# The fourth second product of an MLP by pairs of token blocks, and the attention's division kept clear of the stage behind it

## The chip, the core and the metric

The kernel runs on one core of a Trainium2 chip. The metric is the device time of one execution in microseconds. TensorE (PE) does the matrix products, and its weight loads are shown apart as PEld. VectorE (DVE), ScalarE (ACT) and GpSimd (POOL) do the elementwise work, and SyncE (SP) issues every DMA of this kernel, one behind the other. Lines such as L646 are lines of the kernel before, unless the text says otherwise.

## The reference

The input x has 2048 tokens of 512 features. The output mixes an attention and an MLP of the same x with a gate:

```python
qkv = x @ wqkv                       # 32 heads of 16, scale 16**-0.5
mask = (i - j >= 0) & (i - j < 256)  # sliding window
a = softmax(where(mask, q @ k.T * scale, -1e9)) @ v     # per head
a = a @ wo
b = gelu_tanh(x @ w1 + b1) @ w2 + b2                    # 512 -> 1792 -> 512
g = sigmoid((x * gate_w).sum(-1))
out = g * a + (1 - g) * b
```

All of it is fp32.

## The kernel before, in words

**Dense products.** A dense product takes three matmuls, made by `mm3` (L108 to L110): each operand is split into a rounded part and the rest, and rounded by rounded, rounded by rest and rest by rounded are summed in PSUM. A weight tile therefore comes in as `raw_w` by DMA, ACT copies its rounded part into a `w` tile (L178) and DVE subtracts for the rest (L182). There are 14 `w` buffers and 2 `raw` buffers.

**The MLP in eight stages.** The tokens are cut into four tiles of 512, and the 1792 hidden features into two halves of seven blocks (`HF`). A stage n of the eight in `TURNS` takes one half for one tile: first the "u" part (seven blocks of x by w1, each followed by a chain for gelu on ACT and DVE, L719 to L737, that leaves a tile `h`), then the "y" part (four blocks b of 128 tokens, each the sum over seven i of h by w2). The fourth stage, n = 3, is the last that uses the first half of the weights. During its u part the loads of the second half of w1 are asked for, and in its y part one load of the second half of w2 is asked for behind each of the seven products of block b = 3 (L836). The fifth stage, n = 4, begins with the second half.

**The attention** goes by eight groups g of four heads and, within a group, by four chunks of 512 tokens. For each chunk PE makes row maxima's scores (`sm`, L519), which DVE reduces (`jm` and `M`, L524), then transposed scores (`st`, L564), on which ACT takes the exponential into `pt` (L586) and POOL clears what is outside the window (L580), and then the products with v (L608) into two PSUM tiles, `pv_st` and `pv_sm`. These two come from the same pools as `st` and `sm`, three buffers each. ACT copies the one into a tile `nd` (L629), DVE adds the other (L632), and SP stores the sum to DRAM as ND (L636). A name such as `nd4_1` is group 4, chunk 1.

**The division** (`att_norm`, L642) goes once per chunk and pair of groups, when the second group of the pair is stored: SP loads the denominators from ND (`den`, L646), DVE takes the reciprocal (L650), SP stores them (RD, L653), and later loads the numerators (`num`) and the reciprocals spread over the rows (`rb`, L658); DVE multiplies (L662), and SP stores the quotient (OT, L665), which only the last stage of the program reads. `den1_1`, `num1_1` and `rb1_1` belong to chunk 1 and the second pair of groups, which are groups 2 and 3. There is one `den` buffer, and `nd`, `num` and `rb` take turns in three buffers of one tag, `tmp`: whoever takes a buffer waits for the last reader of its former tile.

**What sets the order.** The order of instructions on each engine, SP among them, is the order in which the program records them; nothing reorders them later. The program keeps a clock of its own in planned nanoseconds. `after(ns, fn)` puts a piece of work on a list, and `tick` runs those whose time has come while PE's work is recorded (`fill` puts dense steps between the attention's). So the delays in the code are planned places in the order, and not waits on the chip. The division's steps are planned at 8, 10, 16, 23 and 25 us from its start (`DIVS`), and its start 6 us (`NORM`) after the store of ND. Weight loads are planned at least 4 us apart (`PACE`), with the split 7.5 us (`LAND`) after the load, and no more than two at a time, since there are two `raw` buffers (`load_now`).

**Semaphores of the DMAs.** SP's transfers use eight completion semaphores in turn, and the order's listing names the ones on which an instruction waits (DMAHW0 to DMAHW7).

## Time and profile before

| | us |
|---|---|
| time, median of 3 runs | 750.57 (749.57 to 752.2) |
| time of the profiled execution | 749.65 |
| span of the profiled execution | 747.9 |
| PE busy in it | 732.7 (98%) |
| DVE busy in it | 520.1 (70%) |
| ACT busy in it | 421.5 (56%) |
| POOL busy in it | 372.3 (50%) |
| share of the DMA queue that SP feeds | 81.4% of 16 engines |

A line of the profile gives a group of instructions or one instruction: its time, its engine, its source line, the tile written and the tiles read, and, in brackets or behind a bar, how long the engine stood idle ahead of it and who released it. Matmuls are pipelined, so a busy PE isn't PE at its peak. The places of this text are given in microseconds from the start of the span. The y part of the fourth stage begins at 391.9, the u part of the fifth at 427.6 and its y part at 463.7.

### The profile page before, as it was taken

How to read it: one execution, taken by the hardware profiler on the slowest of the kernel's cores; microseconds unless marked ns; L12 is line 12 of the kernel's file. 1: busy time of each engine (PE TensorE's matmuls, PEld its weight loads, DVE VectorE, ACT ScalarE, POOL GpSimd, SP SyncE). 2: the span in 40 equal slices, each digit the busy share in tenths (PEclk: the TensorE clock that was granted, in tenths of full speed). 3: DMA queues.
4: the chain of work that ended last, by engine and by line, in shares of the span. 5: the costliest groups of instructions: out<-in, count | busy, mean ns of one | idle time of the engine just before them, and what ended most of it. 6: DMA issues, size and time to landing. Idle time of an engine off the chain costs nothing.

```text
span 747.9 us, 17961 instructions
## 1 busy us (share of the span) xinstructions
PE 732.7 (98%) x6129; PEld 604.4 (81%) x6129; DVE 520.1 (70%) x1567; ACT 421.5 (56%) x972; POOL 372.3 (50%) x846
## 2 busy tenths in 40 slices
PE   8999999998999999999999999999999999999998
PEld 7888888876788888888887877888888888867786
DVE  4532325799768867986798689768867986784552
ACT  4434532358537845864695478438745863794550
POOL 4200000339756865876577568747765875630000
PEclk9999999999999999999999999999999999999999
DMA  9889798998895687899575979996799799468572
GB/s 326 319 272 404 261 391 273 291 293 182 270 259 134 162 243 205 175 222 271 146 179 149 242 211 234 249 237 152 178 256 235 194 224 270 136 181 226 191 252 111
DMA packets 179260, 172.12 MB, mean 230 GB/s; under 512 B 56673, under 2 KB 122977, under 8 KB 179169
## 3 DMA queue, kind: packets, MB, share of 16 engines
q1 hardware_dynamic: 179168, 170.97, 81.4%
q8 instruction: 49, 0.80, 0.5%
q14 instruction: 43, 0.34, 0.1%
HBM read 108.53 MB, written 62.39 MB: 229 GB/s over the span
## 4 chain that ended last, share of the span: by engine, by line
PE 85%; DVE 5%; ACT 3%; issue 3%; DMA 2%; SPq 1%; POOL 1%; DVEq 0%; ACTq 0%
PE sm L519 9%; PE st L564 8%; PE pv_sm L608 7%; PE y L108 7%; PE y L109 6%; PE y L110 6%; PE u L108 5%; PE u L109 5%; PE u L110 5%; PE qk L110 4%; PE qk L108 4%; PE qk L109 4%; PE a L108 2%; DVE jm L524 2%; PE v L108 2%
## 5 line engine op out<-in xcount | busy, mean ns | idle before, releaser
L524 DVE CUSTOM_DVE_ANT_0 jm<-sm,mask 128x320 bf16<-128x320 f32 (+4 forms) x512 | 238.1, 465 | 95.3 <-PE sm L519 61.1
L580 POOL TENSOR_SCALAR_AFFINE_SELECT pt<-pt 64x256 f32<-64x256 f32 (+1 forms) x538 | 227.7, 443 | 108.5 <-ACT pt L586 98.1
L586 ACT ACTIVATE pt<-st 128x320 f32<-128x320 f32 (+4 forms) x512 | 199.6, 424 | 139.1 <-PE st L564 136.0
L519 PE MATMUL sm<-kd,qd 96*128 96x320 f32 (+4 forms) x512 | 153.9, 312 | 6.3 <-DVE M L524 5.5
L564 PE MATMUL st<-qs,ks 128*128 128x320 f32 (+4 forms) x512 | 153.9, 309 | 1.9 <-ACT pt L586 1.9
L546 POOL CAST qs<-tt 4x256 fp32r<-4x256 f32 x256 | 124.6, 487 | 53.3 <-DVE tt L539 42.7
L519 PEld LDWEIGHTS sm<-kd,qd 96*128 96x128 f32 x512 | 96.3, 188 | 33.2 <-DVE M L524 13.7
L564 PEld LDWEIGHTS st<-qs,ks 128*128 128x128 f32 x512 | 97.1, 190 | 18.8 <-ACT pt L586 3.2
L108 PE MATMUL y<-w,h 128*128 128x512 f32 x224 | 88.5, 395 | 0.0
L109 PE MATMUL y<-w,h 128*128 128x512 f32 x224 | 87.9, 393 | 0.0
L110 PE MATMUL y<-w,h 128*128 128x512 f32 x224 | 87.9, 392 | 0.0
L108 PE MATMUL u<-mx,w 128*128 128x512 f32 x196 | 80.0, 408 | 0.0
L109 PE MATMUL u<-mx,w 128*128 128x512 f32 x196 | 77.4, 395 | 0.0
L110 PE MATMUL u<-mx,w 128*128 128x512 f32 x196 | 77.1, 393 | 0.0
L608 PE MATMUL pv_sm<-pt,vbuf 64*32 64x320 f32 (+4 forms) x1408 | 73.6, 346 | 0.2
L608 PE MATMUL pv_st<-pt,vbuf 64*32 64x320 f32 (+4 forms) x1408 | 73.3, 346 | 0.0
L608 PEld LDWEIGHTS pv_sm<-pt,vbuf 64*32 64x32 f32 x1408 | 50.2, 106 | 20.2 <-issue 2.4
L325 DVE TENSOR_TENSOR qke<-qk,qke 128x512 fp32r<-128x512 f32 x32 | 22.0, 688 | 46.9 <-ACT qke L322 33.2
L322 ACT ACTIVATE qke<-qk 128x512 fp32r<-128x512 f32 x32 | 19.1, 597 | 56.2 <-PE qk L110 32.5
L110 PEld LDWEIGHTS y<-w,h 128*128 128x128 f32 x224 | 42.0, 188 | 9.8
L338 POOL MEMSET vx<- 128x32 f32 x16 | 2.4, 156 | 89.0 <-DMA SQ<-qke 44.5
L608 PEld LDWEIGHTS pv_st<-pt,vbuf 64*32 64x32 f32 x1408 | 46.1, 106 | 0.0
(148 smaller groups left out, 1332.7 us busy)
## 6 DMA issues: line engine op xcount, KB each, us to landing
kd<-SK SPq DMA_DIRECT2D x32, 384.0 KB
qs<-SQ SPq DMA_DIRECT2D x64, 192.0 KB
mx<-XT SPq DMA_DIRECT2D x24, 512.0 KB
SQ<-qke SPq DMA_DIRECT2D x16, 512.0 KB
SK<-qke SPq DMA_DIRECT2D x16, 512.0 KB
ND<-nd SPq DMA_DIRECT2D x32, 256.0 KB
raw_w<-in_B_w_dram SPq DMA_DIRECT2D x28, 256.0 KB
ks<-SK SPq DMA_DIRECT2D x32, 192.0 KB
```

The lines of the kernel that those rows point to most:

```text
L108: nc.tensor.matmul(p, lh, rh, start=first, stop=False)
L109: nc.tensor.matmul(p, lh, rl, start=False, stop=False)
L110: nc.tensor.matmul(p, ll, rh, start=False, stop=last)
L322: nc.scalar.activation(e[:, h], p, AF.Copy)
L325: nc.vector.tensor_sub(e[:, 1 - h], p, f32(e[:, h]))
L519: nc.tensor.matmul(p[:, :w], qd[0:96, n, pr, 128 * j:128 * (j + 1)], kd[0:96, n, pr, k1 - w:k1], start=True, stop=True)
L524: nc.vector.tensor_tensor_reduce(junk[:, :w], p[:, :w], mask[:, 320 - w:320], 1.0, -3e38, ALU.add, ALU.max, M[:, 2 * (b % RB) + hb, pr:pr ...
L546: nc.gpsimd.tensor_copy(dst, src.unsqueeze(1).broadcast_to([4, 2, RB, 32]))
L564: nc.tensor.matmul(p[:, :w], ks[:, slot(g_, kb // NB), pr, at:at + 128], qs[:, pr, k0:k0 + w], start=True, stop=True)
L580: nc.gpsimd.affine_select(out=v, in_=v, pattern=[[0, v.shape[1]], [1 - 2 * e, 64]], compare_op=ALU.is_ge, fill=0.0, base=-e, channel_multi ...
L586: nc.scalar.activation(pt[:, hf, pr, :w], p[:, :w], AF.Exp, scale=SCALE)
L608: nc.tensor.matmul(pv[r // 64][32 * i:32 * i + 32, q - c * T:e - c * T], vts[g_, b // NB][r:r + 64, v:v + 32], rhs(r), start=start, stop=s ...
```

## The change

There are two edits. The y part of the fourth stage (n = 3) takes its 28 products in another order: block 0 and block 1 alternate from the fourth product on, then block 2 and block 3 likewise, where before only three products of block 1 stood ahead of block 0's last one, and blocks 2 and 3 came whole, one behind the other. Behind each product of block 3 a load of w2 is asked for, as before.

And the division is no longer started straight away 6 us after the store of ND. It goes through `norm`, which puts it off by 1 us again and again while `heavy` is set (from the beginning of that y part to the third block of the fifth stage's u part), and which starts two divisions at least 11 us of planned time apart (`APART`). `heavy` is never set elsewhere, and the last four divisions of the program don't go through `norm`.

```diff
--- before.py
+++ after.py
@@ -636,8 +636,21 @@
             nc.sync.dma_start(ND[c][g_ // 2][g_ % 2], nd)
             done.add(("nd", g_, c))
             if g_ % 2 == 1:
-                after(NORM if g_ * NT + c < NQ - 4 else 3500, att_norm, c, g_ // 2)
+                if g_ * NT + c < NQ - 4:
+                    after(NORM, norm, c, g_ // 2)
+                else:
+                    after(3500, att_norm, c, g_ // 2)
         after(100, half), after(700, ev)
+
+    norms = [0.0]
+
+    def norm(t, c):
+
+        at = max(now[0], norms[0])
+        if heavy[0]:
+            return after(1000, norm, t, c)
+        norms[0] = at + APART
+        after(at - now[0], att_norm, t, c)
 
     def att_norm(t, c):
 
@@ -739,6 +752,7 @@
         for ns, fn in zip(GELU, (f1, f2, f3, f4, f5, f6)):
             after(ns, fn)
 
+    heavy = [False]
     yas = {}
 
     def ya_load(k):
@@ -787,6 +801,8 @@
             hs.append(h)
             if last and later:
                 load(later.pop(0))
+            if n == NT:
+                heavy[0] = i < 2
         if n == 0:
             for c in range(NC):
                 nc.sync.dma_start(XT[t][c], f32(xt[:, c]))
@@ -823,8 +839,16 @@
 
 
         stage[0] = "y"
-        turns = [(0, i) for i in range(HF - 1)] + [(1, i) for i in range(YSWAP)] + [(0, HF - 1)]
-        turns += [(1, i) for i in range(YSWAP, HF)] + [(b, i) for b in range(2, NB) for i in range(HF)]
+        if n == NT - 1:
+            turns, heavy[0] = [], True
+            for b in range(0, NB, 2):
+                turns += [(b, i) for i in range(YSWAP)]
+                for i in range(YSWAP, HF):
+                    turns += [(b + 1, i - YSWAP), (b, i)]
+                turns += [(b + 1, i) for i in range(HF - YSWAP, HF)]
+        else:
+            turns = [(0, i) for i in range(HF - 1)] + [(1, i) for i in range(YSWAP)] + [(0, HF - 1)]
+            turns += [(1, i) for i in range(YSWAP, HF)] + [(b, i) for b in range(2, NB) for i in range(HF)]
         for b, i in turns:
             ts = slice(b * 128, (b + 1) * 128)
             if i == 0:
@@ -1002,6 +1026,7 @@
 GELU = (700, 1500, 3600, 4600, 6000, 7000)
 XAT = 3
 ORDER = 'mspf'
+APART = 11000.0
 XOR = 1
 PACE = 4000.0
 LAND = 7500.0
```

In the changed file the lines from `att_norm` to the end of `gelu` are higher by 13 (den L659, RD L666, num and rb L671, OT L678, mx L690, the gelu chain L732 to L750); those above are the same.

**DVE at the end of the fifth stage's u part.** Before, these rows follow one another; `jm` and `M` are one reduction of the score tile `sm`, and `w2_13` is the split of the last w2 tile:

```order
L524 ISA jm5_2_1_6706,M5_0_6520<-sm5_2_1_6704,mask_72 128x320
L524 ISA M5_0_6520 128x1
L524 ISA jm5_2_0_6722,M5_0_6520<-sm5_2_0_6720,mask_72 128x320
L524 ISA M5_0_6520 128x1
L182 TENSOR_TENSOR w2_13_6718<-raw_w213_6562,w2_13_6718 128x512
L524 ISA jm5_2_3_6734,M5_0_6520<-sm5_2_3_6732,mask_72 128x320
L524 ISA M5_0_6520 128x1
L731 SCALAR_TENSOR_TENSOR x1h2_12_6669_6675<-sqh2_12_6669_6676,x1h2_12_6669_6675 128x512
```

Now:

```order
L524 ISA jm5_2_1_6683,M5_0_6498<-sm5_2_1_6681,mask_72 128x320
L524 ISA M5_0_6498 128x1
L524 ISA jm5_2_0_6699,M5_0_6498<-sm5_2_0_6697,mask_72 128x320
L524 ISA M5_0_6498 128x1
L524 ISA jm5_2_3_6710,M5_0_6498<-sm5_2_3_6708,mask_72 128x320
L524 ISA M5_0_6498 128x1
L744 SCALAR_TENSOR_TENSOR x1h2_12_6647_6653<-sqh2_12_6647_6654,x1h2_12_6647_6653 128x512
L524 ISA jm5_2_2_6728,M5_0_6498<-sm5_2_2_6726,mask_72 128x320
```

The split of `w2_13` no longer stands among these reductions; it stands 16 rows ahead of the first row shown, and the splits of the other w2 tiles of this half have moved ahead likewise.

**SP from the y part of the fifth stage on.** Before, `RD3_1` is the store of the last of the four divisions, `mx40` parts of the next tile of x, `qs`, `kd` and `qd` loads of the attention:

```order
L653 DMA RD3_1_128<-den3_1_6494 128x32 [waits DMAHW1_49,DVE_49]
L677 DMA mx40_6739<-XT0_91 128x1024 [waits DMAHW2_49,PE_49]
L499 DMA qs_73<-SQ0_79 48x2x512 [waits DMAHW3_49]
L499 DMA qs_73<-SQ0_79 48x2x512 [waits DMAHW4_49]
L658 DMA num3_1_6814<-ND3_1_112 128x1x512 [waits DMAHW5_49]
L658 DMA rb3_1_6816<-RD3_1_128 128x1x512 [waits DMAHW7_49,DMAHW6_49,DMAHW1_49]
L677 DMA mx40_6739<-XT0_91 128x1024
L488 DMA kd_76<-SK1_84 96x2x256 [waits DMAHW0_49]
L488 DMA kd_76<-SK2_85 96x2x512 [waits PE_49]
L480 DMA qd_75<-SQ2_81 48x8x128 [waits DMAHW2_49]
L475 DMA qd_75<-SQ2_81 48x7x128 [waits DMAHW3_49]
L477 DMA qd_75<-SQ2_81 48x2x64 [waits DMAHW4_49]
```

Now the division of chunk 2 stands here, that of chunk 0 begins, and the store of chunk 1's quotient comes behind the loads:

```order
L690 DMA mx40_6715<-XT0_91 128x1024 [waits DMAHW6_49,PE_49]
L499 DMA qs_73<-SQ0_79 48x2x512 [waits DMAHW7_49]
L499 DMA qs_73<-SQ0_79 48x2x512 [waits DMAHW0_49]
L666 DMA RD2_1_124<-den2_1_6602 128x32 [waits DMAHW1_49,DVE_49]
L659 DMA den0_1_6795<-ND0_1_100 128x1x32 [waits DMAHW2_49,DMAHW1_49]
L690 DMA mx40_6715<-XT0_91 128x1024 [waits DMAHW3_49]
L488 DMA kd_76<-SK1_84 96x2x256 [waits DMAHW4_49]
L488 DMA kd_76<-SK2_85 96x2x512 [waits DMAHW5_49,PE_49]
L480 DMA qd_75<-SQ2_81 48x8x128 [waits DMAHW6_49]
L475 DMA qd_75<-SQ2_81 48x7x128 [waits DMAHW7_49]
L477 DMA qd_75<-SQ2_81 48x2x64 [waits DMAHW0_49]
L678 DMA OT1_96<-num1_1_6693 128x512 [waits DVE_49]
```

Of the divisions of these four chunks, which before started in the order 0, 1, 2, 3 during the fourth stage's y part and the fifth's u part, that of chunk 1 now starts first, behind the third block of the fifth stage's u part, and then those of chunks 2, 0 and 3. The load of `den0_1` waits for the store of RD that stands right ahead of it, since both use the one `den` buffer.

**ACT at the copy of `nd4_1`.** Before:

```order
L586 ACTIVATE pt4_8_6826<-st4_8_2_6858 128x320 [waits PE_49]
L629 ACTIVATE nd4_1_6918<-pv4_1_st_6863 128x512 [waits DMAHW0_49,PE_49]
L586 ACTIVATE pt4_8_6826<-st4_8_3_6923 128x320 [waits PE_49]
L586 ACTIVATE pt4_9_6950<-st4_9_0_6951 128x320 [waits PE_49,Pool_49]
L586 ACTIVATE pt4_9_6950<-st4_9_1_6958 128x320 [waits PE_49]
```

Now:

```order
L586 ACTIVATE pt4_8_6802<-st4_8_2_6835 128x320 [waits PE_49]
L629 ACTIVATE nd4_1_6900<-pv4_1_st_6840 128x512 [waits DMAHW1_49,DVE_49,PE_49]
L586 ACTIVATE pt4_8_6802<-st4_8_3_6905 128x320 [waits PE_49]
L586 ACTIVATE pt4_9_6931<-st4_9_0_6932 128x320 [waits PE_49,Pool_49]
L586 ACTIVATE pt4_9_6931<-st4_9_1_6939 128x320 [waits PE_49]
```

The copy takes a `tmp` buffer. Before, the last reader of that buffer was the store of an ND; now it is the store of `OT1_96` of the fence ahead, which uses DMAHW1, and which stands 8 rows of SP ahead of the store of `nd4_1` itself.

## The prediction, as it was put on record

> **What bounds the kernel now.** The page comes first.

> ```profile
> span 747.9 us, 17961 instructions
> PE 732.7 (98%) x6129; PEld 604.4 (81%) x6129; DVE 520.1 (70%) x1567; ACT 421.5 (56%) x972; POOL 372.3 (50%) x846
> ```

> PE is the bound; only what makes PE wait counts. [...] What PE waited for over the span, from the view of waits:

> ```profile
> PE sm L519 <- DVE M L524: 5.5, 11, 1.0
> PE st L564 <- ACT pt L586: 1.9, 3, 1.2
> ...
> PE a L108 <- DVE ao L879: 0.2, 1, 0.2
> ```

> The columns are total us, count and longest; these are the first two and the last of eight rows. The largest is the wait for the row maxima, 5.5 of 747.9 us, and none of the eight is a y or u matmul that waits for a weight tile. The places of the change were then read by stretches: an untouched y stage, the y part of the fourth stage, and the u and y parts of the fifth.

> ```profile
> core 0: us, PE busy (x) PEld busy (x) DVE busy (x) ACT busy (x) POOL busy (x), PEclk, DMA share, GB/s
> 288.90:323.60 34.70, 34.70 (x324) 28.82 (x323) 29.63 (x95) 26.93 (x61) 24.74 (x52) 1.00 0.75 167
> 391.90:427.80 35.90, 34.69 (x343) 28.61 (x342) 27.36 (x91) 18.27 (x44) 25.31 (x61) 1.00 0.74 184
> 427.80:463.50 35.70, 34.64 (x317) 27.59 (x317) 32.03 (x97) 28.27 (x64) 24.52 (x48) 1.00 0.85 223
> 463.50:498.00 34.50, 33.77 (x339) 27.58 (x338) 25.35 (x86) 16.47 (x40) 23.78 (x59) 1.00 1.00 255
> ```

> The granted clock is full. DVE is fullest in 427.8 to 463.5 (32.03 of 35.70). The DMA engines are fullest in the stretch behind it (1.00, 255 GB/s): that is where the divisions go. PE's waits in the three last stretches, the first row from 391.9 to 427.8, the next two from 427.8 to 463.5, the last from 463.5 to 498:

> ```profile
> PE sm L519 <- DVE M L524: 1.2, 2, 0.9
> ...
> PE sm L519 <- DVE M L524: 0.4, 2, 0.3
> PE sm L519 <- DVE nd L632: 0.4, 1, 0.4
> ...
> PE sm L519 <- DVE M L524: 0.6, 1, 0.6
> ```

> All six end on DVE, 2.6 us. That is all that this change can win here.

> **The change part by part. Turns by pairs.** The 28 products and their matmuls are the same, so PE work changes by 0. Block 3's products come four products earlier, and so each of the seven w2 loads and splits. As PE waits for no weight, the earlier buffers alone bring 0; the cover is that no such wait is there. What they do is take DVE work out of the end of the fifth stage's u part:

> ```profile
> 440.75 0.75 DVE L662 TENSOR_TENSOR num<-num,rb 128x512 f32<-128x512 f32 x1 [0.48 <-DMA rb<-RD]
> 443.58 0.42 PE L519 MATMUL sm<-kd,qd 96*128 96x320 f32 x1 [0.26 <-DVE M L524]
> 458.69 0.36 PE L519 MATMUL sm<-kd,qd 96*128 96x192 f32 x1 [0.43 <-DVE nd L632]
> 460.10 0.89 DVE L662 TENSOR_TENSOR num<-num,rb 128x512 f32<-128x512 f32 x1
> 461.32 0.41 PE L519 MATMUL sm<-kd,qd 96*128 96x320 f32 x1 [0.17 <-DVE M L524]
> 464.85 0.69 DVE L182 TENSOR_TENSOR w<-raw_w,w 128x512 fp32r<-128x512 f32 x1
> 465.86 0.69 DVE L731 SCALAR_TENSOR_TENSOR x1h<-sqh,x1h 128x512 f32<-128x512 f32 x1
> 466.88 0.85 DVE L725 SCALAR_TENSOR_TENSOR sqh<-sqh,x1h 128x512 f32<-128x512 f32 x1
> 467.11 0.32 PE L519 MATMUL sm<-kd,qd 96*128 96x320 f32 x1
> 467.26 0.31 PE L564 MATMUL st<-qs,ks 128*128 128x320 f32 x1
> 468.19 0.41 PE L519 MATMUL sm<-kd,qd 96*128 96x320 f32 x1 [0.62 <-DVE M L524]
> ```

> Three of these waits have a cause that moves. At 468.19 PE waits behind the split of w2_13 at 464.85 (0.69 us) and two gelu steps; without the split, the 0.62 goes. At 443.58 and 461.32 it waits 0.26 and 0.17 behind a division's multiply (440.75, 460.10), which moves. The wait at 458.69 stays: the order puts w2_13 where w2_12 stood, beside that `nd`. A wait is longer than its bracket, since a matmul of 0.31 us follows its forerunner after 0.15 (467.11, 467.26): 0.16 is hidden each time. Gain: 0.26 + 0.17 + 0.62 + 3 x 0.16 = **1.5 us**. Its bounds: 0, if other DVE work falls on the same places, and 2.6 + 6 x 0.16 = 3.6, if all six waits go.

> **The division moved.** Its instructions are the same and each issue costs SP the same; it leaves DVE idle earlier and busy later, and the multiplies come where DVE has 9 us free (25.35 of 34.50). Its transfers move into the stretch where the DMA share is 1.00. Two waits are new there. The load of `den0_1` has to wait for RD2's landing (one buffer), and so holds all of SP; and the copy of `nd4_1` on ACT has to wait for OT1's landing, since the `tmp` buffer that it takes is now num1's. Behind that copy stand the exponentials on ACT, and PE's fourth `st` behind it needs the PSUM tile that the copy frees. Rows of before for this place:

> ```profile
> 433.07 7.66 DMA rb<-RD
> 447.88 3.07 DMA raw_w<-in_B_w_dram
> ...
> 474.83 0.60 ACT L629 ACTIVATE nd<-pv_st 128x512 f32<-128x512 f32 x1 [1.94 <-PE pv_sm L608]
> 475.54 0.68 DVE L632 TENSOR_TENSOR nd<-nd,pv_sm 128x512 f32<-128x512 f32 x1
> ...
> 476.91 0.31 PE L564 MATMUL st<-qs,ks 128*128 128x320 f32 x1
> ...
> 462.64 0.40 SPq L653 DMA_DIRECT2D RD<-den  x1
> 463.61 0.32 SPq L677 DMA_DIRECT2D mx<-XT  x1
> ...
> 466.29 0.45 SPq L677 DMA_DIRECT2D mx<-XT  x1
> 466.79 2.16 SPq L488 DMA_DIRECT2D kd<-SK  x2
> 468.99 0.45 SPq L480 DMA_DIRECT2D qd<-SQ  x1
> ...
> 470.51 0.43 SPq L677 DMA_DIRECT2D mx<-XT  x1
> ```

> The first two are transfers of 0.26 MB in the chain that ended last, with issue to landing: 3.07 us in a calm queue, 7.66 in a loaded one. SP's rows give about 0.5 us for an issue.

> *Landing of RD2.* It is issued behind `num1`, `rb1`, a part of mx (463.61, 0.8 us earlier by the gain up to there: 462.8) and two loads of qs, so at 464.3. By the calm row it lands at 467.4; by the loaded one, counted from `rb1` at 462.1, rb1 lands at 469.8, and behind it come mx and qs, 0.92 MB at 255 GB/s = 3.6 us, 473.4. I take 471, since rb1, the slow one, stands ahead of it.

> *Landing of OT1.* Then come den0, mx, kd, kd, three qd and OT1. The seven issues after den0 take 3.5 us. Their bytes are 0.52 + 0.20 + 0.39 + 0.20 + 0.17 + 0.03 + 0.26 = 1.77 MB, at 255 GB/s 6.9 us, and the calm row leaves 3.07 - 0.26/0.255 = 2.0 us beside the bytes. From the issue of mx at 471.6: 471.6 + 6.9 + 2.0 = 480.5. The bounds from RD2's go from 476.9 to 482.9. SP also waits for the transfer eight issues before its own; before, that cost 2.1 us in this place, and it can only make OT1 later:

> ```profile
> SPq L480 <- DMA rb<-RD: 2.1, 1, 2.1
> ```

> *The stall A.* The copy ends 0.6 us later, at 481.1. The `st` that needs it would come at 476.91 - 1.5 = 475.4. **A = 5.7 us**, between 2.1 and 8.1. [...]

> *Behind it, B and C.* The same happens to `nd4_2`, one chunk later: nd4_0's add ended near 458.69, nd4_1's at 476.22, so the pitch is 17.5 and nd4_2's copy is due at 474.83 + 17.5 + 4.2 = 496.5. It waits for OT2. SP stores nd4_1 at about 481.8, then RD0, and is held at den3 until that lands (3.07 to 7.66 later: 485 to 489.5); six more issues, 3 us, then OT2 lands 3.07 to 7.66 later: 491 to 500. B is 0 to 3.5. C is the fuller queue: 1.5 divisions more in the last stretch, each 3 x 0.26 MB at 255 GB/s = 3.1 us, so 0 to 4.7, for the loads are asked for a chunk (17.5 us) ahead. I take 2.0 for both, nearer to the low ends, with 0 and 5 as bounds.

> The wait of den2 for RD1 near 455 costs SP up to 7.66 us too, and holds the loads of ks behind it; the cover is again that chunk ahead, and I put it at 0, and at what exceeds 17.5 us if it is gone.

> Sum against the profiled execution, 749.65: - 1.5 + 5.7 + 2.0 = 755.85. The median of the runs shown is 0.92 above that execution, so **756.8 us**.

> **The rivals.** *Clean gain.* OT1 lands ahead of the copy, as its like did before. For it: the copy then waited only for PE (1.94, 474.83). Against it: OT1 would have to land by 474.8, and even the low bound is 476.9. The time is 749.65 - 1.5 + 0.92 = 749.1, and with all six waits gone 747.0. It decides if SP isn't held at den0 for more than 2 us. What counts as faster, below, needs a gain over 2.25.

> *A small stall.* RD2 lands early and the queue is emptier than its share says: A is 2.1 to 3, B and C 0, so the time is 751.2 to 752.1, no change. For it: the calm row. Against it: 1.00 and 7.66.

> *A second stall of the same size.* `nd4_2` waits as long as `nd4_1`: with B at 3.5 and C at 4.7 instead of 2.0 it is 763.0. For it: two more divisions cross the same full stretch. Against it: after the first stall everything has 4.2 us more.

> *The change doesn't do what it says.* The splits move but others take their place, no wait goes: the gain is 0 and the time 1.5 higher with A, 758.3. It lies in the likeliest case's range.

> **How the numbers follow.** A measurement of this kernel can't tell less than about 0.3%, 2.25 us, from no change: 748.3 to 752.8. The likeliest case (stall A, 753 to 761) has 0.64; the small stall 0.12 and the clean gain at 749.1 0.04, both no change; the clean gain with more waits gone 0.10, faster; the second stall 0.10. So faster 0.10, no change 0.16, slower 0.74. The range of 8 in 10 reaches from 750.0, where the small stall begins, to 763.5 behind the second.

> **What would show it.** In the changed kernel's profile: PE waits of several us at `st` L564 between 475 and 482, put down to ACT; ACT's `nd` L629 there with idle time ended by the DMA of OT; SP waiting at `den` for the DMA of RD; the stretch from 463.5 longer by 6 or more us, the one from 427.8 shorter by about 1; no wait at 468.19. The prediction is wrong if `nd4_1`'s copy waits for PE alone, or if the time comes from a load of `ks`, `kd` or `mx` that is late.

## The result, and the profile after

The changed kernel takes 760.61 us in the median of 6 runs (757.08 to 761.95), the kernel before 750.74 us beside it (749.57 to 752.2). The ratio is 1.013, with a 95% interval of 1.0106 to 1.0155: it is slower, as forecast, by 9.9 us where 6.2 were forecast, and inside the range of 750.0 to 763.5. Its profiled execution is the fastest of the six, 757.08 us; the five others lie between 760.3 and 762.0, and that spread has a cause of its own, below.

The page after: the span, the busy times, and the two groups that changed.

```profile
span 755.4 us, 17970 instructions
PE 734.3 (97%) x6129; PEld 606.1 (80%) x6129; DVE 520.6 (69%) x1567; ACT 421.8 (56%) x972; POOL 370.7 (49%) x846
...
L564 PE MATMUL st<-qs,ks 128*128 128x320 f32 (+4 forms) x512 | 154.6, 310 | 8.3 <-ACT nd L629 6.1
...
L629 ACT ACTIVATE nd<-pv_st 128x512 f32<-128x512 f32 x32 | 19.1, 597 | 50.9 <-PE pv_sm L608 35.9
```

No engine is busier than before. The idle time ahead of `st` has grown from 1.9 to 8.3 us, and 6.1 of it is put down to ACT's `nd`. The waits of PE over the span (total us, count, longest) say that it is one wait:

```profile
PE st L564 <- ACT nd L629: 6.1, 1, 6.1
PE sm L519 <- DVE M L524: 5.5, 10, 1.0
```

The stretches, with the granted clock (the share of its full clock that TensorE was granted) in the third column from the end. The last is taken longer, since the stage ends later:

```profile
427.80:463.50 35.70, 35.39 (x326) 29.20 (x325) 32.70 (x101) 29.13 (x66) 24.61 (x50) 1.00 0.80 186
463.50:505.00 41.50, 34.84 (x334) 28.67 (x333) 25.42 (x87) 15.37 (x39) 21.97 (x56) 0.92 0.80 213
```

The first of the two is better filled than before (PE busy 35.39 instead of 34.64, and 9 matmuls more done in it): the gain is there. In the other the clock is no longer 1.00. The place itself, first in the timeline (start, us, engine, instruction, in brackets the idle time ahead of it and who ended it), with the rows of SP, ACT and PE one behind the other:

```profile
469.99 0.59 SPq L659 DMA_DIRECT2D den<-ND  x1
...
474.18 0.43 SPq L678 DMA_DIRECT2D OT<-num  x1
...
480.39 0.60 ACT L629 ACTIVATE nd<-pv_st 128x512 f32<-128x512 f32 x1 [9.62 <-DMA OT<-num]
...
466.06 0.41 PE L519 MATMUL sm<-kd,qd 96*128 96x320 f32 x1 [0.56 <-DVE M L524]
...
481.04 0.64 PE L564 MATMUL st<-qs,ks 128*128 128x320 f32 x1 [6.10 <-ACT nd L629]
```

And in the waits of SP between 450 and 500:

```profile
SPq L659 <- DMA RD<-den: 9.4, 3, 4.7
```

This is the forecast chain: SP is held 4.7 us at the load of `den0_1`, which goes at 469.99; OT1 goes at 474.18; the copy of `nd4_1` has waited 9.62 us for its landing and starts at 480.39; PE's `st` comes at 481.04 after 6.10 us of idle time. The matmul at 466.06 is the one that stood at 468.19 before, so the kernel was 2.1 us ahead there.

Behind the stall PE runs at half its clock (columns: PE busy, weight loads, DVE, ACT, POOL, then clock, DMA share, GB/s):

```profile
478.00:479.00 1.00, 0.00 (x0) 0.00 (x0) 0.00 (x0) 0.00 (x0) 0.00 (x0) 0.86 1.13 335
479.00:480.00 1.00, 0.00 (x0) 0.00 (x0) 0.00 (x0) 0.00 (x0) 0.00 (x0) 0.50 1.11 373
...
485.00:486.00 1.00, 1.00 (x4) 0.73 (x4) 0.01 (x1) 0.00 (x0) 0.95 (x3) 0.72 1.00 275
486.00:487.00 1.00, 1.00 (x7) 0.94 (x6) 0.50 (x3) 0.49 (x2) 0.18 (x1) 1.00 0.48 114
```

To book the time, I compare the starts of the same `st` matmul in both traces. Up to 468 the changed kernel is 2.1 us ahead. Behind the stall it is 6.3 us late, so the stall costs 8.4: 6.1 of idle time, and 2.3 for the 4.5 us in which PE works at 0.50. Near 510 comes 1.3 more. The sum, -2.1 + 8.4 + 1.3 = 7.6, is but for 0.2 the difference of the profiled executions, 757.08 - 749.65 = 7.4.

### The profile page after: what moved, and what is told of

Same layout as the page of the kernel before. It is cut to its first block, busy times and chain, and to the rows that moved or that the text cites. A ratio compares the mean times of both kernels' runs of the same rounds, so it can differ in the third digit from the quotient of the medians.

```text
span 755.4 us, 17970 instructions
## 1 busy us (share of the span) xinstructions
PE 734.3 (97%) x6129; PEld 606.1 (80%) x6129; DVE 520.6 (69%) x1567; ACT 421.8 (56%) x972; POOL 370.7 (49%) x846
## 4 chain that ended last, share of the span: by engine, by line
PE 85%; DVE 4%; ACT 3%; DMA 3%; issue 3%; SPq 1%; POOL 1%; DVEq 0%; ACTq 0%; POOLq 0%
PE sm L519 9%; PE st L564 8%; PE pv_sm L608 7%; PE y L108 6%; PE y L109 6%; PE y L110 6%; PE u L108 6%; PE u L109 5%; PE u L110 5%; PE qk L110 4%; PE qk L108 4%; PE qk L109 4%; PE a L108 2%; PE v L108 2%; PE v L110 2%
## 5 line engine op out<-in xcount | busy, mean ns | idle before, releaser
L524 DVE CUSTOM_DVE_ANT_0 jm<-sm,mask 128x320 bf16<-128x320 f32 (+4 forms) x512 | 238.1, 465 | 94.3 <-PE sm L519 59.8
L586 ACT ACTIVATE pt<-st 128x320 f32<-128x320 f32 (+4 forms) x512 | 199.6, 425 | 138.8 <-PE st L564 135.3
L564 PE MATMUL st<-qs,ks 128*128 128x320 f32 (+4 forms) x512 | 154.6, 310 | 8.3 <-ACT nd L629 6.1
L519 PE MATMUL sm<-kd,qd 96*128 96x320 f32 (+4 forms) x512 | 153.8, 312 | 6.0 <-DVE M L524 5.5
L519 PEld LDWEIGHTS sm<-kd,qd 96*128 96x128 f32 x512 | 96.6, 189 | 31.8 <-DVE M L524 11.9
L564 PEld LDWEIGHTS st<-qs,ks 128*128 128x128 f32 x512 | 97.5, 191 | 25.7 <-ACT nd L629 6.4
L108 PE MATMUL y<-w,h 128*128 128x512 f32 x224 | 89.2, 398 | 0.0
L108 PE MATMUL u<-mx,w 128*128 128x512 f32 x196 | 80.0, 408 | 0.0
L608 PE MATMUL pv_sm<-pt,vbuf 64*32 64x320 f32 (+4 forms) x1408 | 73.6, 346 | 0.1
L608 PE MATMUL pv_st<-pt,vbuf 64*32 64x320 f32 (+4 forms) x1408 | 73.3, 346 | 0.0
L608 PEld LDWEIGHTS pv_sm<-pt,vbuf 64*32 64x32 f32 x1408 | 50.2, 106 | 20.2 <-issue 2.2
L629 ACT ACTIVATE nd<-pv_st 128x512 f32<-128x512 f32 x32 | 19.1, 597 | 50.9 <-PE pv_sm L608 35.9
```

The lines of the kernel that those rows point to most:

```text
L108: nc.tensor.matmul(p, lh, rh, start=first, stop=False)
L519: nc.tensor.matmul(p[:, :w], qd[0:96, n, pr, 128 * j:128 * (j + 1)], kd[0:96, n, pr, k1 - w:k1], start=True, stop=True)
L524: nc.vector.tensor_tensor_reduce(junk[:, :w], p[:, :w], mask[:, 320 - w:320], 1.0, -3e38, ALU.add, ALU.max, M[:, 2 * (b % RB) + hb, pr:pr ...
L564: nc.tensor.matmul(p[:, :w], ks[:, slot(g_, kb // NB), pr, at:at + 128], qs[:, pr, k0:k0 + w], start=True, stop=True)
L586: nc.scalar.activation(pt[:, hf, pr, :w], p[:, :w], AF.Exp, scale=SCALE)
L608: nc.tensor.matmul(pv[r // 64][32 * i:32 * i + 32, q - c * T:e - c * T], vts[g_, b // NB][r:r + 64, v:v + 32], rhs(r), start=start, stop=s ...
```

## The experiments

Each run was taken beside runs of the kernel before on the same chip; the ratios are to those, with their 95% intervals in brackets. Runs on different chips are compared by their ratios. The diffs show the lines that matter; "..." stands for lines left out.

**The turns alone.** The division starts as before:

```diff
-                if g_ * NT + c < NQ - 4:
-                    after(NORM, norm, c, g_ // 2)
-                else:
-                    after(3500, att_norm, c, g_ // 2)
+                after(NORM if g_ * NT + c < NQ - 4 else 3500, att_norm, c, g_ // 2)
```

> The pair turns alone, the divisions started as before. Theory (all of the loss is one stall of PE: ACT's copy of nd4_1 waits for the landing of OT1, and the granted clock is low for some 5 us behind it): the copy waits for PE alone, the wait of 0.62 us at 468.19 behind the split of w2_13 goes, so 0 to 1 us faster than before: 749.5 to 751. Rival (the turns themselves cost, by crowding weight loads): about 757 to 760.

Measured: 750.27 us in the median against 750.12, ratio 1.0004 (0.9988 to 1.0021). The turns cost nothing and bring nothing that can be measured. By the starts in the trace this kernel is 0.5 us ahead at 468. It was 0.4 us behind already from 160 on, where both kernels are the same, so from 391.9 on the turns win 0.9 us, but not where I expected it. PE's instruction there, in this run's timeline:

```profile
467.71 0.41 PE L519 MATMUL sm<-kd,qd 96*128 96x320 f32 x1 [0.61 <-DVE M L524]
```

The matmul of 468.19 still waits 0.61 us, although the split of w2_13 is no longer among DVE's work ahead of it. The two gelu steps there (0.69 and 0.85 us, with the reductions behind them) are enough.

**The division alone.** The fourth stage has its old turns:

```diff
-            turns, heavy[0] = [], True
+            heavy[0] = True
+            turns = [(0, i) for i in range(HF - 1)] + [(1, i) for i in range(YSWAP)] + [(0, HF - 1)]
+            turns += [(1, i) for i in range(YSWAP, HF)] + [(b, i) for b in range(2, NB) for i in range(HF)]
```

> The division put off as in the changed kernel, the fourth stage's turns as before. Theory: the same stall of about 6 us at the copy of nd4_1 with a low clock behind it, plus the 0.6 to 0.8 us at w2_13's split that the turns would have taken away: 758 to 762. Rival (the turns cost): near 750.

Measured: 759.21 us, ratio 1.0118 (1.0085 to 1.0151). Its trace has the same stall, by the waits of PE from 463.5 to 520:

```profile
PE st L564 <- ACT nd L629: 6.1, 1, 6.1
```

So the whole loss belongs to the division that was put off, and the turns have no part in it. At 468 this kernel is 1.6 us ahead; counted from 391.9, where it was 0.5 us behind, it wins 2.1. The changed kernel wins 2.2 from there (2.2 to 2.6 in the seven traces with the same work up to 468), so the shares of the division and of the turns don't simply add.

**A buffer of its own for `nd`.** One of the three `tmp` buffers goes to `nd`, two stay for `num` and `rb` (the loads of x for the last stage, which use these buffers too, are shared out likewise):

```diff
-        nd = sb.tile([128, T], F32, tag="tmp", bufs=3, name=f"nd{g_}_{c}")
+        nd = sb.tile([128, T], F32, tag="nd", bufs=1, name=f"nd{g_}_{c}")
...
-                tiles.append(sb.tile([128, T], F32, tag="tmp", bufs=3, name=f"{name}{t}_{c}"))
+                tiles.append(sb.tile([128, T], F32, tag="tmp", bufs=2, name=f"{name}{t}_{c}"))
```

> The changed kernel, with one of the three buffers of tmp given to nd alone, and the other two to num and rb; SP is still held at den0 for RD2, and rb2 now has to wait for OT1. Theory: the copy of nd4_1 waits for PE alone, the stall and the low clock behind it go, and what is left is the gain: 748.5 to 751. Rival (SP's being held at the den loads, and with it late loads, costs the time): still 756 to 761.

Measured: 760.24 us, ratio 1.0117 (1.0093 to 1.0141). My expectation missed, and the rival, a late load behind SP's being held, comes nearer. The copy of `nd4_1` waits for PE alone now, but the wait for OT1 has only moved to the load of `rb2`. The waits of SP between 455 and 510 in this run:

```profile
SPq L671 <- DMA OT<-num: 9.5, 2, 5.2
```

And one instruction each of DVE and PE in its timeline:

```profile
484.16 0.69 DVE L675 TENSOR_TENSOR num<-num,rb 128x512 f32<-128x512 f32 x1 [5.25 <-DMA rb<-RD]
...
485.32 0.63 PE L519 MATMUL sm<-kd,qd 96*128 96x320 f32 x1 [4.16 <-DVE M L524]
```

SP is held 5.2 us at the load of `rb2`, DVE stands at the multiply for it, the reductions stand behind the multiply, and PE waits 4.16 us for a reduction, with the half clock behind it. In both arrangements of the buffers someone waits for OT1.

**Two `den` buffers.** This takes away SP's wait for RD2; the space for it comes from the table `cut`, which is bf16 now:

```diff
-        den = sb.tile([128, 32], F32, tag="den", bufs=1, name=f"den{t}_{c}")
+        den = sb.tile([128, 32], F32, tag="den", bufs=2, name=f"den{t}_{c}")
...
-    cut = cs.tile([128, 2, 64], F32, name="cut")
+    cut = cs.tile([128, 2, 64], BF16, name="cut")
```

> The changed kernel with two den buffers (96 bytes for it come from the table cut, now bf16), so that den0 no longer waits for RD2 and SP isn't held 4.7 us there; the copy of nd4_1 still waits for OT1. Theory (OT1 is late since its issue is late): OT1 is issued some 4 to 5 us earlier and lands at 475 to 477, the stall is 0.5 to 2 us: 750.5 to 753.5. Rival (the queue is full, and OT1 lands at 479 to 480 whenever it is issued): the stall stays 5 to 6 us, 757 to 761.

Measured: 751.38 us, ratio 1.0019 (0.9992 to 1.0046); nine of ten executions lie between 749.4 and 754.9, one at 759.61 (its mean clock is 0.993, as in the stalled executions of the changed kernel). The waits of PE from 463.5 to 520 show that the stall has shrunk:

```profile
PE st L564 <- ACT nd L629: 1.5, 1, 1.5
```

The mean clock of the execution is 1.0. OT1's issue and the copy in this run:

```profile
470.65 0.34 SPq L678 DMA_DIRECT2D OT<-num  x1
...
476.49 0.60 ACT L629 ACTIVATE nd<-pv_st 128x512 f32<-128x512 f32 x1 [5.02 <-DMA OT<-num]
```

OT1 goes 3.5 us earlier than in the changed kernel, and the copy starts 3.9 us earlier. (The rest of the 4.6 us by which the stall is shorter is that PE was 0.7 us later in this execution.) So OT1 was late because SP was held, and not because the queue was full whenever it was issued; from its issue to the copy it takes 5.8 us here and 6.2 there. This is the change's first cause: the 11 us between two divisions' starts leave 1 us between the store of RD (10 us after the start) and the load of the next `den` into the same buffer.

**PE kept busy over the wait, and the changed kernel again.** The score matmul ahead of the waiting `st` is issued 40 times, with the same result; the wait for OT1 stays.

```diff
+        for _ in range(40 if (g_, b, i) == (5, 5, 0) else 1):
-        nc.tensor.matmul(p[:, :w], qd[0:96, n, pr, 128 * j:128 * (j + 1)], kd[0:96, n, pr, k1 - w:k1],
+            nc.tensor.matmul(p[:, :w], qd[0:96, n, pr, 128 * j:128 * (j + 1)], kd[0:96, n, pr, k1 - w:k1],
...
```

> The changed kernel, where the score matmul that stands ahead of the waiting st (0.15 us each) is issued 40 times over into the same tile, so that PE is busy during the some 6 us in which it waits for the copy of nd4_1. The wait for OT1 stays as it is. Theory (of the 8.4 us lost there, 6.1 are the wait and 2.3 the granted clock of 0.5 behind it): the clock stays at 1.0, and the time is 2 to 3 us below the changed kernel's, 754.5 to 758. Rival (the low clock belongs to the work behind the wait, not to the idle time): no gain, 757 to 762.

> The changed kernel once more, as a base for the run ahead, and for a second trace: its six executions lay at 757.1 once and at 760.3 to 762.0 five times. If the place where the low clock begins makes that difference, the stall is the same 6 us and the clock of 0.5 lies wholly on busy time, up to 3.4 us instead of 2.3. If a second wait makes it, the trace shows another idle time of PE of 2 to 4 us.

Measured: 761.93 us (ratio 1.0148, 1.0126 to 1.017) with PE kept busy; 760.51 us (1.012, 1.0093 to 1.0148) for the changed kernel. In the first the clock holds at the stall, as two stretches over the stall and behind it show (the clock is the third column from the end):

```profile
478.00:480.00 2.00, 2.00 (x16) 2.00 (x15) 0.00 (x0) 0.00 (x0) 0.00 (x0) 1.00 1.00 330
...
482.00:484.00 2.00, 2.00 (x11) 1.76 (x12) 1.86 (x7) 1.49 (x5) 1.56 (x4) 1.00 1.01 196
```

The stall costs 6.1 us by the `st` starts there, instead of 8.4: the 2.3 is the clock's. But the gain is given back in the next 30 us (2.0 near 497 and 1.5 near 510, where the changed kernel's profile has 0 and 1.3): near 497 DVE stands 1.84 us at a multiply for `rb`, and PE behind it. Nor is the clock full everywhere in this kernel: the mean of the traced execution is 0.998, although the stretches read from 470 to 496 and from 512 to 528 all have 1.00, and the mean clocks of the four executions are 0.995 to 0.998.

The second trace of the changed kernel is an execution of 760.57 us, and shows what makes the spread. Its stall at `nd4_1` is 6.6 us long. Near 516, DVE stands at the last division's multiply, and PE behind it. The timeline of the first trace:

```profile
514.66 0.69 DVE L675 TENSOR_TENSOR num<-num,rb 128x512 f32<-128x512 f32 x1 [2.86 <-DMA rb<-RD]
...
516.42 0.41 PE L519 MATMUL sm<-kd,qd 96*128 96x320 f32 x1 [0.45 <-DVE M L524]
```

That of the second:

```profile
516.52 0.69 DVE L675 TENSOR_TENSOR num<-num,rb 128x512 f32<-128x512 f32 x1 [4.10 <-DMA rb<-RD]
...
518.28 0.42 PE L519 MATMUL sm<-kd,qd 96*128 96x320 f32 x1 [1.69 <-DVE M L524]
```

And the second trace's stretches there:

```profile
518.00:520.00 2.00, 1.41 (x6) 0.93 (x6) 1.71 (x5) 2.00 (x5) 0.58 (x2) 0.95 1.14 251
520.00:522.00 2.00, 2.00 (x6) 1.71 (x7) 1.86 (x8) 1.67 (x4) 1.71 (x4) 0.50 1.14 324
522.00:524.00 2.00, 2.00 (x10) 1.86 (x9) 1.49 (x5) 0.87 (x2) 0.35 (x1) 0.69 1.05 216
```

When DVE's wait for `rb` is 1.2 us longer, PE waits 1.69 us instead of 0.45, the clock falls a second time, and the place costs 4.0 us instead of 1.3. The mean clocks of the ten executions of the changed kernel fit this: 0.995 in the two at 757, and 0.992 or 0.993 in seven of the eight at 760 and more (the eighth has 0.996).

**The last multiply later.** Two runs test that: the changed kernel with one multiply recorded behind 7 more reductions, and, as the price of the low clock was still mixed with the second stall, the same with PE kept busy as above.

```diff
+        late = 4000 if (t, c) == (3, 1) else 0
         for ns, fn in zip(DIVS[c == NC - 1], (rcp, keep, back, mul, store)):
-            after(ns, fn)
+            after(ns + late * (fn in (mul, store)), fn)
```

> The changed kernel with the multiply and the store of the last of the four divisions (chunk 3) recorded 4 us of planned time later, behind 7 more reductions of DVE. Theory (the executions at 760 us and more are those in which rb of that division lands later, DVE stands at the multiply, PE waits 1.7 us for the row maxima and the clock falls once more): the wait near 516 is gone and with it the spread, and all executions lie at 755.5 to 757.5. Rival (the spread comes from the first stall): the median stays at 760 to 761.

> Both edits on the changed kernel: the score matmul issued 40 times ahead of the waiting st, and the last multiply 4 us later. With PE kept busy alone the median was no lower than the changed kernel's, since the second stall was still in it; without that stall the price of the low clock stands alone. Theory (2 to 3 us of the first stall are the clock of 0.5 behind it): 2 to 3 us below the run with the late multiply alone (756.46), 753.5 to 755. Rival (the low clock costs nothing, as what it delays had slack): 756 to 757.

Measured: 756.46 us (756.1 to 759.05; ratio 1.0083, 1.006 to 1.0107) for the first. PE has no wait between 505 and 520, and three of four executions lie within 0.7 us. All four have a mean clock of 0.995. So the second stall makes most of the difference between 757 and 761: 2.8 of 3.5 us between the two traces of the changed kernel (0.8 is there already from 160 on).

With PE kept busy as well: 757.67 us (754.96 to 761.55; 1.0071, 1.0049 to 1.0093). The intervals overlap, so no gain is shown. The three fastest of its seven executions (754.96 to 755.46) lie 0.6 to 1.1 us below the fastest without it, the others above. Its trace, an execution at 761.55, has 3.7 us from an undisturbed part of the kernel near 205, no loss to the clock at the stall, and 3.9 us behind it, at what is 497 in the kernel before. Only part of that is a new wait; the half clock comes back behind it, as one row of the timeline and one stretch show (the kernel's lines are higher by one in this run):

```profile
505.91 0.41 PE L520 MATMUL sm<-kd,qd 96*128 96x320 f32 x1 [1.72 <-DVE M L525]
...
507.45:510.86 3.41, 3.41 (x12) 2.83 (x11) 2.46 (x9) 0.72 (x3) 0.82 (x2) 0.50 0.92 182
```

DVE had stood 2.58 us at the multiply for `rb` ahead of it. The six other executions have a mean clock of 0.999 or 1.000, and still lie between 754.96 and 757.89. That the low clock costs 2.3 us where it stands is shown; that its removal would shorten the kernel is not. In the two traces with PE kept busy, waits for `rb`, and in the second the half clock behind one, took the gain back.

**More room between the divisions.** APART is 16000 instead of 11000, with the pair turns and with the old ones:

```diff
-APART = 11000.0
+APART = 16000.0
```

> The changed kernel with APART = 16000 instead of 11000: each division's transfers fall between two copies of nd, so that nd4_1 takes the buffer of nd4_0, and den0 is loaded 4 us or more behind the store of RD2. Theory: no wait of ACT for an OT, no stall, the gain of 2.1 us up to 468.19 stays, and some of the 1.1 us near 510: 748.5 to 750.5. Rival (the divisions' transfers in the full stretch cost by themselves): 752 or more.

> As the run before, with the old turns in the fourth stage's y part. Theory: the shares of the gain add up, 1.6 us of the moved divisions and 0.5 of the turns, so this is 0.5 us slower than with the pair turns: 749 to 751. Rival (the turns are worth nothing, or the gain is theirs): the same as with the pair turns, or as the kernel before.

Measured: 750.14 us against 750.68 (0.9992, 0.9975 to 1.0009) with the pair turns, and 748.98 us (0.9978, 0.9968 to 0.9988) with the old ones. Neither has a wait of ACT for an OT, nor a low clock at this place: with one number of the change its loss is gone. That the old turns do no worse here went against my expectation; that they do better is not shown, since the intervals overlap. In the traces the pair turns lose it near 508, where PE waits 1.45 us for a reduction, behind a multiply that waits 3.90 for `rb`; with the old turns the multiply waits 2.83. Why `rb` is later with the pair turns was not tried. Some 0.5 us of the gain lies elsewhere, in all three traces with 16000: near 324, ahead of the fourth stage's y part, since APART spaces the earlier divisions too.

**And later multiplies.** The same, with the old turns:

```diff
+        late = {mul: 2500, store: 1500} if c == 1 else {}
         for ns, fn in zip(DIVS[c == NC - 1], (rcp, keep, back, mul, store)):
-            after(ns, fn)
+            after(ns + late.get(fn, 0), fn)
```

> APART = 16000, the old turns, and the four divisions' multiplies recorded 2.5 us and their stores 1.5 us of planned time later. Theory (what is left in that kernel is DVE standing 2.8 us at a multiply for rb near 504, which takes back about 1 us of its gain): 747 to 748.5, 0.3 to 0.4% faster than the kernel before. Rival (the multiplies then stand at places where DVE is full): 749 to 751.

Measured: 748.25 us against 751.02, ratio 0.997 (0.9955 to 0.9985), with a span of 746.5 in the profiled execution. This is the lowest median of the study, and faster than before; that it is faster than the run without the later multiplies is not shown, since the intervals overlap. One division's multiply still waits 2.47 us for `rb`.

## Why the prediction was right, and where it was not

The direction and the cause were right: the copy of `nd4_1` waits for OT1, since SP is held at `den0` and a buffer has another last reader. The steps:

- *RD2's landing, 471, and OT1's, 480.5.* The load behind RD2 went at 469.99, and the copy started at 480.39. That the second is right to 0.1 us is partly luck: RD2 was 1.0 us earlier than taken, and the way from there to OT1's landing took 10.4 us instead of 9.5.
- *The stall A, 5.7.* The wait is 6.1. The term was too small nevertheless, and this is the step of the sum that failed, since a whole price was missing: the granted clock falls during the wait, and PE works at 0.50 for 4.5 us behind it, 2.3 us. The stall costs 8.4. I wrote that the clock is full, and did not ask what a wait would do to it. In this trace the clock falls 3.8 us into the idle time, at 478.72.
- *B and C, 2.0 with bounds 0 and 5.* The size holds: 1.3 in the one trace, 4.0 in the other. The place failed. `nd4_2`'s copy has no such wait in either; what waits is DVE, at the last division's multiply, for `rb` (2.86 and 4.10 us). What failed here is the sentence that the multiplies come where DVE has 9 us free. Free time on average is no cover for an instruction that stands in order and waits for a transfer, with the row maxima behind it.
- *The gain, 1.5.* It is 2.1 at 468. The wait at 468.19 that was to go with w2_13's split stayed (0.56); the one at 458.69 that was to stay went, as did those at 443.58 and 461.32. Counted from 391.9 it is 2.2, and alone the division wins 2.1 and the turns 0.9, so most of it doesn't need the turns. The size came out near by errors of place that partly cancelled. One reading of the change was wrong too: only the first of block 3's products comes four places earlier, and the last three stand where they stood. The loads of w2 were still issued earlier, the first at 412.0 instead of 417.2 and the last at 445.0 instead of 454.0.
- *The 0.92 between the profiled execution and the median.* It was taken over from before. In the changed kernel it is 3.5, since the profiled execution fell on a short second wait; which execution is profiled is chance. A stall whose length depends on a transfer's landing has a spread, and the sum of one trace doesn't see it. This is the larger part of what the forecast of 756.8 lacks to 760.61.
- *The rivals.* The clean gain and the small stall didn't come; the small stall is what two `den` buffers make of it (1.5 us). A second stall did come, on another engine, and smaller than the 763.0 of that rival.

## What to carry to other kernels

When work is put off, follow its buffers, and not only its instructions: who takes the buffer next, and for which transfer it will then wait. Two delays that are sums of planned times (here 10 us to the store of RD and 11 us to the next load into the same buffer) can meet: SP stood 9.4 us in three such waits between 450 and 500; 16 instead of 11 took the loss of 1.3% away, and left a gain of 0.2% with the old turns. A wait of PE like those of 4.2 to 6.6 us here is to be priced with the slow clock behind it (2.3 us where it was measured alone; what the whole kernel would win without it is not shown), and an instruction that waits for a transfer is to be moved behind the work that could go first.

## What the runs showed of the hardware

```profile
484.00:485.00 1.00, 0.00 (x0) 0.00 (x0) 0.84 (x2) 0.00 (x0) 0.00 (x0) 0.76 1.10 310
...
491.00:492.00 1.00, 1.00 (x6) 0.81 (x5) 0.00 (x0) 0.00 (x0) 0.52 (x2) 0.83 0.85 307
```

A shorter wait can have the half clock behind it as well. In the changed kernel's second trace the clock fell again at 519.81, behind a wait of 1.69 us (516.59 to 518.28), and was low for 3.42 us, to 523.23; the half clock from 507.45 to 510.86, with PE kept busy and the last multiply later, came behind a wait of 1.72. Behind a wait of 1.45 us in the run with APART = 16000 (506.74 to 508.19) the clock stayed at 1.00, and with two `den` buffers the mean clock is 1.0 with a wait of 1.5. In the profile of the kernel before the longest wait of PE is 1.2 us, and the clock is 1.00 in every stretch. First the rows around the wait of 1.69 us, then, in the other run, those around the wait of 1.45 us:

```profile
516.40:519.81 3.41, 1.45 (x6) 0.79 (x5) 3.00 (x7) 1.96 (x5) 0.39 (x2) 1.00 1.08 294
519.81:523.23 3.42, 3.37 (x10) 3.08 (x11) 3.14 (x11) 2.39 (x7) 1.90 (x5) 0.50 1.08 271
...
505.00:507.00 2.00, 1.74 (x43) 0.96 (x27) 0.78 (x2) 0.00 (x0) 0.00 (x0) 1.00 1.14 252
507.00:509.00 2.00, 0.81 (x4) 0.76 (x5) 1.88 (x7) 0.02 (x1) 1.15 (x2) 1.00 0.90 222
509.00:512.00 3.00, 2.67 (x12) 1.73 (x12) 2.56 (x9) 3.00 (x7) 2.69 (x6) 1.00 0.70 179
```

In the 3.41 us ahead of the fall PE is idle for 1.96 us; in the four from 505 to 509 in the other run for 0.26 and 1.19, 1.45 together. These few waits don't tell how long PE has to be idle for the clock to fall, and no run was made to test it.
